# Mamba2 scan and gated feed-forward layer on one core: the first block's steps rearranged, with causal masks on GpSimd for pairs 1 to 3

## The chip, the core and the metric

The kernel runs on one core of a Trainium2 chip. The metric is the time on the device in microseconds (us). Three runs of the kernel before the change took 409.44, 410.94 and 410.81 us, median 410.81.

## What is computed

The reference has two parts. The first is a state-space scan (batch 4, 8 heads, sequence 768, head size 32, state size 16). The reference's chunks are 32 long; any chunk length gives the same sums.

```
log_a = log(clip(a, 1e-6, 1));  cum = cumsum(log_a within a chunk)
L[i,j] = exp(cum[i] - cum[j]) for i >= j, else 0
y      = ((C B^T) * L) x  +  exp(cum) * (C state)
state  = exp(sum log_a) * state + sum_j exp(cum[last] - cum[j]) B_j x_j
```

Its output, 3072 tokens of 256 features, goes into the second part: `xn = y / sqrt(mean(y^2) + 1e-6) * rms_g`, then `silu(xn w_gate) * (xn w_val)`, times `w_out`, with a hidden width of 1536. All weights come in float32.

## The kernel before the change

The 3072 tokens are 12 pairs of 128-token chunks; two pairs make a block of 512 tokens, and there are six blocks. While the feed-forward part of a block runs on TensorE (PE), the scan of the next block is worked out between its matmuls. Block 0 has nothing before it, so its scan (pairs 0 and 1) comes first: this is the lead-in. In it the weights are also brought in: `fetch.k` loads a piece, `pow.k` (ACT, three activations, L182 to L185), `man.k` and `wt.k` (VectorE, DVE, L192, L195, L201) turn it into the form in which it is used. There are 20 pieces: 0 to 3 of 256 columns, 4 to 13 of 512 (gate and value), 14 to 19 of w_out.

**The order is written out by hand.** A long string at the end of the kernel lists steps such as `0:g.0.1/0` (block 0, step g, pair 0, half 1, PSUM slot 0). The kernel emits each step's instructions in that order, and every engine and every DMA queue takes its own in that order. SP issues nearly all DMAs. There are three PSUM slots of two banks (`pair_of_banks`) in the lead-in and two single banks (`bank`), used in turn; a slot is free again when its last reader is done. The raw weights (`wr`) share six buffers.

The steps of a pair, with their lines:

- `aT` (L303) turns a onto tokens, `la0` (L307) clips it, `log`, `log4` (L312, L344) take logarithms. `r` (L355) sums them, `parts` (L362 to L369) splits the sums into three bfloat16 parts, rows.
- `mask` (L422) puts a huge negative number above the diagonal into the bank `e`, by a matmul with a unit matrix. `sums` (L436, L443) adds the sums of logarithms, with small tiles of 32 rows. `exp` (L451) makes the decays L of them. Pairs 0 and 1 have L of 128x1024 for each half of the heads; pairs 2 and 3 work with chunks of 64 and one L of 128x1024.
- `d`, `dx` (L379, L382, L387) are the decays to and from a token; `c`, `cx`, `cc` (L396 to L408) those of whole chunks, of which `cc` makes the column fcol. `scale` (L484) puts them on C and B.
- `turn`, `T`, `Tt` (L499, L507, L1034, L1037) turn B and C, with masks for the two heads of a row tile; `last`, `Tl` (L517, L521) the scaled C.
- `g` (L529; L536 for later pairs) is C B^T: each group of two heads (q = 0 to 3) is one row tile of 32 rows. For pairs 0 and 1 each half has a step of its own, with two row tiles. `L` (L556) multiplies it by the decays.
- `A`, `S` (L582, L596 to L606) are additions to the state and the states. `y` (L623 with the state, L632 within the chunk; L656 for later pairs) is the output, `sq` and `yt` (L695, L712) its squares and its copy to SBUF.

After that `early` (L770) multiplies y by the first gate and value weights before the norm is known, `gate` (L760) does this for normed tokens (`norm` L781, `xn` L741), and from `P` (L844) on products of combined weights and tokens follow, seven where there were eight (`cw` L814, `tx` L821, `two` L890, with `take` L850, `C` L856, `silu` L865, `hid` L869). `o` (L876) and `O` (L934) are the products with w_out. For pairs from 4 on the decays L come by another way: `spread` loads rows of sums by DMA, `sub` (L463) and `ex` (L469) finish them, and GpSimd masks them (L471):

```
        nc.scalar.activation(out=L, in_=L, func=AF.Exp)
        for r in halves:
            nc.gpsimd.affine_select(out=L[r], in_=L[r], pattern=[[0, NH], [1, HC]],
                                    compare_op=ALU.is_ge, fill=0.0, base=0, channel_multiplier=-1)
```

Of the kernel before, what the change touches and what calls it, by code (L numbers as in the profile page):

```python
# [13 lines left out]
BF16 = mybir.dt.bfloat16  # L14
AF = mybir.ActivationFunctionType
# [5 lines left out]
def kernel(  # L21
# [199 lines left out]
    never16 = const.tile([P, HC], BF16, name="never16")  # L221
# [65 lines left out]
    def mask16():  # L287
        for r in halves:
            nc.vector.tensor_copy(out=never16[r], in_=never[r, r])

# [26 lines left out]
    def minus_mid():  # L317
# [19 lines left out]
        "ident16": lambda: nc.vector.tensor_copy(out=ident16, in_=ident), "never16": mask16,  # L337
# [38 lines left out]
    def other_sums():  # L376
# [4 lines left out]
        for k, (r, m) in enumerate((halves, halves[::-1])):  # L381
            nc.tensor.matmul(out=d_ps[m, k, first_four[0], first_four[1]], lhsT=ones[r, m],  # L382
                             rhs=la[(r, *first_four)], start=False, stop=True,
                             tile_position=(r.start, m.start), skip_group_check=True)

    def other_decays():
        nc.scalar.activation(out=d_sb, in_=ps.pop("d"), func=AF.Exp)  # L387

# [3 lines left out]
    def chunk_sums():  # L392
        ps["c"] = full_ps = bank("full_ps", (P, NG * NH))
        n = NC * BH
        for u in range(2):
            nc.tensor.matmul(out=full_ps[:, u * n:u * n + n], lhsT=chunk_ones[:, u], rhs=laf,  # L396
                             start=(u == 0), stop=True, skip_group_check=True)
        nc.tensor.matmul(out=full_ps[:, 2 * n:].rearrange("p (c h) -> p c h", h=NH), lhsT=ones,
                         rhs=la[(slice(0, P), *first_four)], start=False, stop=True,
                         skip_group_check=True)  # L400

    def chunk_decays():
        nc.scalar.activation(out=full.rearrange("p g h -> p (g h)"), in_=ps.pop("c"), func=AF.Exp)
# [15 lines left out]
    def mask(p, e):  # L419
        m = [P, 4, P] if p < 2 else [P, NH, HC]  # L420
        for i in range(2):
            nc.tensor.matmul(out=e[:, i], lhsT=ident16,  # L422
                             rhs=(whole16 if p < 2 else never16).unsqueeze(1).to_broadcast(m),
                             start=True, stop=False, skip_group_check=True)

    def sums(p, half, e):
# [5 lines left out]
        row = rows[p // 2]  # L432
        for k, h in enumerate(heads):
            for i, r in enumerate(rows_of):
                for u in parts:
                    nc.tensor.matmul(out=e[u, i, k * n:(k + 1) * n],  # L436
                                     lhsT=sel[r, h:h + 1].to_broadcast([32, n]),
                                     rhs=row[r, 0, u], start=False, stop=False,
                                     tile_position=(r.start, u.start), skip_group_check=True)
        hs = slice(heads[0], heads[-1] + 1)  # L440
        for i, r in enumerate(rows_of):
            for u in parts:
                nc.tensor.matmul(out=e[u, i], lhsT=row[r, 1, u],  # L443
                                 rhs=sel[r, hs].unsqueeze(2).to_broadcast([32, len(heads), n]),
                                 start=False, stop=True, tile_position=(r.start, u.start),
                                 skip_group_check=True)

    def decay(p, half, e):
        pair_tile(2 * p)
        L = Ls[p][:, :, 4 * half:4 * half + 4] if p < 2 else Ls[p]  # L450
        nc.scalar.activation(out=L.rearrange("p i h m -> p i (h m)"), in_=e, func=AF.Exp)  # L451

# [88 lines left out]
    def products(p, half, g):  # L541

        ps["g", p, half] = g
        product(p, [(2 * half + k, g[:, k]) for k in range(2)])

    def products_at_once(p, g):

        ps["g", p, 0] = g
        ps["g", p, 2], ps["g", p, 3] = g2, g3 = bank("g2", (P, 512)), bank("g3", (P, 512))
# [63 lines left out]
    def first_outputs(p, y):  # L613
# [4 lines left out]
        def inter(i, opens):  # L618
            S, CdT = state[2 * (2 * p + i) - 1], s["T"][:, i, 3]
            for q in range(NQ):  # L620
                r = slice(32 * q, 32 * q + 32)
                o = 64 * (q % 2)
# [3 lines left out]
                    start=opens, stop=True, tile_position=(32 * q, o),  # L626
                    skip_group_check=True)

        def intra(i, opens):
            for h in range(NH):  # L630
# [3 lines left out]
                    rhs=Ls[p][:, i, h], start=opens, stop=True,  # L634
                    tile_position=(0, o), skip_group_check=True)

        if p:
            inter(0, True)
        intra(0, p == 0)
        intra(1, False)  # L640
# [677 lines left out]
```

## Time and profile before

| | |
|---|---|
| median of the runs | 410.81 us |
| the profiled execution | 409.49 us |
| its span, first to last instruction | 407.4 us |
| PE busy | 399.9 us (98%) |
| DVE busy | 303.7 us (75%) |
| ACT busy | 231.9 us (57%) |
| GpSimd (POOL) busy | 37.5 us (9%) |
| first `early` matmul | at 26.18 us |

Matmuls overlap one another, so a PE that counts as busy is not always at its peak. Times of instructions are given as start and length in us from the span's start. "x8" in a timeline line means eight instructions put together, and [0.96 <-...] that the engine stood idle for 0.96 us before, and what seems to have released it.

### The profile page before, as it was taken

To read this page: it belongs to the slowest core of one execution; us is meant where nothing else is said; L and a number is where in the kernel's file an instruction comes from. 1 tells how busy PE (TensorE), PEld (TensorE's weight loads), DVE (VectorE), ACT (ScalarE), POOL (GpSimd) and SP (SyncE) were. 2 spreads that over 40 slices of the span, in tenths; PEclk is the share of its full clock that TensorE was granted. 3 is DMA by queue.
4 is the path that set the end of the run, shared out by engine and by line. 5 is a ranking of instruction groups with operands and counts; after the bars stand their busy time and mean duration, and the time that the engine had idled before them with its cause. 6 is when DMAs were issued, how large, how long until landed. Compare 5 with 4: busy or idle time off the path is not lost.

```text
span 407.4 us, 9550 instructions
## 1 busy us (share of the span) xinstructions
PE 399.9 (98%) x3867; PEld 340.4 (84%) x3867; DVE 303.7 (75%) x698; ACT 231.9 (57%) x506; POOL 37.5 (9%) x61
## 2 busy tenths in 40 slices
PE   8999999999899999999999999999999999999997
PEld 4566577888688899888899988899988899988997
DVE  5999999898976787856799278779455777265863
ACT  3899989795556445664584355534566442453500
POOL 4010000003200001300023000001300000000000
PEclk9999999999999999999999999999999999999999
DMA  9998937400401171302080501020300000100001
GB/s 112 231 213 173 266 118 209 53 0 5 75 0 28 29 126 39 44 1 55 20 131 8 79 2 53 2 80 2 77 2 0 2 4 0 53 1 2 0 2 52
DMA packets 87371, 23.91 MB, mean 59 GB/s; under 512 B 76800, under 2 KB 81152, under 8 KB 87328
## 3 DMA queue, kind: packets, MB, share of 16 engines
q1 hardware_dynamic: 83168, 23.05, 26.9%
q10 hardware_dynamic: 4160, 0.26, 0.8%
q8 instruction: 30, 0.49, 0.5%
q14 instruction: 13, 0.11, 0.1%
HBM read 20.02 MB, written 3.28 MB: 57 GB/s over the span
## 4 chain that ended last, share of the span: by engine, by line
PE 90%; DVE 4%; ACT 3%; DMA 1%; issue 1%; SPq 0%; ACTq 0%
PE gate L844 27%; PE o L934 22%; PE val L844 20%; PE o L876 4%; PE gate L760 3%; PE y L656 3%; PE tp L499 2%; PE gate L770 2%; PE g L536 1%; PE ms L725 1%; DVE sw L814 1%; DVE s L907 1%; DMA L<-rowd 1%; PE e L422 1%; ACT e L183 1%
## 5 line engine op out<-in xcount | busy, mean ns | idle before, releaser
L856 DVE TENSOR_TENSOR c<-val,p 128x512 f32<-128x512 f32 x99 | 67.6, 688 | 46.3 <-PE val L844 27.5
L850 ACT COPY p<-gate 128x512 f32<-128x512 f32 x99 | 57.4, 586 | 52.4 <-PE gate L844 49.2
L844 PE MATMUL gate<-tx,sw 128*128 128x256 f32 x264 | 65.5, 381 | 0.0
L865 ACT ACTIVATE c<-c 128x256 f32<-128x256 f32 x99 | 39.9, 417 | 41.8 <-DVE c L856 41.6
L844 PEld LDWEIGHTS gate<-tx,sw 128*128 128x128 f32 x264 | 49.1, 190 | 7.0 <-ACT p L850 0.3
L869 DVE TENSOR_TENSOR h<-c 128x256 f32<-128x256 f32 x99 | 41.4, 433 | 17.4 <-ACT c L865 17.3
L844 PE MATMUL val<-tx,sw 128*128 128x256 f32 x132 | 33.9, 381 | 1.2 <-DVE c L856 1.2
L844 PE MATMUL val<-xn,wgv 128*128 128x256 f32 x132 | 34.1, 380 | 0.0
L844 PE MATMUL gate<-xn,wgv 128*128 128x256 f32 x132 | 34.0, 382 | 0.0
L844 PE MATMUL val<-xn,sw 128*128 128x256 f32 x132 | 33.9, 381 | 0.0
L844 PE MATMUL gate<-tx,wgv 128*128 128x256 f32 x132 | 33.8, 383 | 0.0
L471 POOL TENSOR_SCALAR_AFFINE_SELECT L<-L 64x512 f32<-64x512 f32 x32 | 23.5, 734 | 83.3 <-ACT L L469 72.9
L934 PEld LDWEIGHTS o<-two,s 128*128 128x128 f32 x240 | 28.3, 192 | 1.9 <-issue 1.4
L934 PE MATMUL o<-wo,h 128*128 128x128 f32 x240 | 29.5, 275 | 0.0
L934 PE MATMUL o<-two,s 128*128 128x128 f32 x240 | 29.3, 276 | 0.1
L934 PEld LDWEIGHTS o<-wo,h 128*128 128x128 f32 x240 | 28.4, 192 | 0.7 <-DVE h L869 0.2
L934 PE MATMUL o<-two,h 128*128 128x128 f32 x240 | 28.9, 275 | 0.0
L844 PEld LDWEIGHTS val<-tx,sw 128*128 128x128 f32 x132 | 24.7, 190 | 5.0 <-DVE c L856 1.6
L844 PEld LDWEIGHTS gate<-tx,wgv 128*128 128x128 f32 x132 | 24.4, 190 | 4.2 <-ACT p L850 0.6
L934 PEld LDWEIGHTS o<-two,h 128*128 128x128 f32 x240 | 27.8, 192 | 0.0
L844 PEld LDWEIGHTS val<-xn,wgv 128*128 128x128 f32 x132 | 24.5, 190 | 3.9 <-DVE c L856 0.6
L844 PEld LDWEIGHTS val<-xn,sw 128*128 128x128 f32 x132 | 24.6, 190 | 3.5 <-DVE h L869 0.2
(179 smaller groups left out, 645.9 us busy)
## 6 DMA issues: line engine op xcount, KB each, us to landing
L<-rowd SPq DMA_DIRECT2D x32, 128.0 KB, 3.2
xr<-in_x_dram SPq DMA_DIRECT2D x24, 128.0 KB, 4.2
wr<-in_moe_w_out_dram SPq DMA_DIRECT2D x6, 512.0 KB, 5.0
wr<-in_moe_w_gate_dram SPq DMA_DIRECT2D x5, 512.0 KB, 5.8
wr<-in_moe_w_val_dram SPq DMA_DIRECT2D x5, 512.0 KB, 5.9
out_dram<-ob SPq DMA_DIRECT2D x9, 256.0 KB, 2.2
br<-in_B_dram SPq DMA_DIRECT2D x22, 64.0 KB, 3.8
cr<-in_C_dram SPq DMA_DIRECT2D x22, 64.0 KB, 3.1
```

What stands on the lines that cost most here:

```text
L471: nc.gpsimd.affine_select(out=L[r], in_=L[r], pattern=[[0, NH], [1, HC]], compare_op=ALU.is_ge, fill=0.0, base=0, channel_multiplier=-1)
L499: nc.tensor.transpose(out=tp[:, k], in_=src[:, i].rearrange("p h n -> p (h n)"), identity=ident)
L656: nc.tensor.matmul(out=y[2 * k + u][rows, i * HC:(i + 1) * HC], start=(k, u, rows.start) not in opened, stop=True, skip_group_check=True, ...
L760: nc.tensor.matmul(out=gv[:, k], lhsT=w[:, t, fs], rhs=xns[0][:, t], start=(t == 0), stop=(t == 1))
L770: nc.tensor.matmul(out=gv[:, k, tk], lhsT=w[:, t, fs], rhs=yts[0][:, t, tk], start=(s == 0 and t == 0), stop=(t == 1), skip_group_check=True)
L844: nc.tensor.matmul(out=dst[:, half[w]], lhsT=lhsT, rhs=rhs, start=(k in (1, 2, 5) and w == 0), stop=True, skip_group_check=True)
L850: nc.scalar.copy(out=t, in_=Xs[j])
L856: nc.vector.tensor_tensor(out=t, in0=Zs[j], in1=a, op=ALU.add)
L865: nc.scalar.activation(out=u, in_=src[:, half[0]], func=AF.Silu)
L869: nc.vector.tensor_tensor(out=hidden_tile(blk, j)[:, c // 10 - 1, c % 10 - 1], in0=u, in1=src[:, half[1]], op=ALU.mult)
L876: nc.tensor.matmul(out=o, lhsT=hs_[blk, f // 2][:, f % 2, k // 2, (k % 2) * P:(k % 2 + 1) * P], rhs=wo[:, f], start=opens, stop=(f == NF - ...
L934: nc.tensor.matmul(out=o[t] if apart else o[:, t * P:(t + 1) * P], lhsT=lhsT[:, t], rhs=rhs, start=(k in (1, 2, 4, 5) and j == 0 and (apar ...
```

## The change

1. For pairs 0 and 1, `g` is one step: the products of all four row tiles of a pair, into two PSUM slots.
2. Only pair 0 is masked by matmuls. For pairs 1 to 3 `mask` is left out, the first matmul of `sums` opens the bank, and a new step `keep` sets the upper triangle of L to zero on GpSimd after `exp`: two selects of 128x512 for each half of pair 1, four of 64x512 for pairs 2 and 3. In `sums` the two kinds of matmul change places. The bfloat16 mask of 64 columns, never16, is gone.
3. The two matmuls in `d` and the one in `c` that join half chunks for pairs 0 and 1 are gone; GpSimd multiplies the decays instead (`dd`, and one product in `cx`).
4. In `y` of pairs 0 and 1 all products with the state come ahead of those within the chunk. Pair 1's additions (`A.1`) are done at the end of `y.0`, into a part of its bank.
5. `T` and `Tt` of pair 0 are made by ACT instead of DVE.
6. The order is new, in all six blocks. In the lead-in `aT` stands between pair 0's two masks; `fetch.18`, `x.3` stand earlier, `bc.3`, `bc.4` and `bc.5` in other places, `rowout.1` ahead of `fetch.8`; `scale.2` stands behind `yt.0`. Around the border to block 1, `sub.8` to `sub.10`, `cw.2` and `two.0` stand behind more of block 1's products. Blocks 1 to 5 have the same steps as before in another sequence.

The diff's core, with the order up to the first products of pair 3:

```diff
-        for k, (r, m) in enumerate((halves, halves[::-1])):
-            nc.tensor.matmul(out=d_ps[m, k, first_four[0], first_four[1]], lhsT=ones[r, m],
-                             rhs=la[(r, *first_four)], start=False, stop=True,
-                             tile_position=(r.start, m.start), skip_group_check=True)
...
+    def of_other_half():
+        for u, r in enumerate(halves[::-1]):
+            first = d_sb[(r, u, *first_four)]
+            nc.gpsimd.tensor_tensor(out=first, in0=first, in1=first_groups(r, u), op=ALU.mult)
...
     def chunk_sums():
-        ps["c"] = full_ps = bank("full_ps", (P, NG * NH))
         n = NC * BH
+        ps["c"] = full_ps = bank("full_ps", (P, 2 * n))
         for u in range(2):
             nc.tensor.matmul(out=full_ps[:, u * n:u * n + n], lhsT=chunk_ones[:, u], rhs=laf,
                              start=(u == 0), stop=True, skip_group_check=True)
-        nc.tensor.matmul(out=full_ps[:, 2 * n:].rearrange("p (c h) -> p c h", h=NH), lhsT=ones,
-                         rhs=la[(slice(0, P), *first_four)], start=False, stop=True,
-                         skip_group_check=True)
+
+    def first_groups(r, u):
+        return full[r, 0:NG - 4].rearrange("p (u c b) h -> p u c b h", u=2, b=NB)[:, u, 0:4, 0]
...
-        nc.scalar.activation(out=full.rearrange("p g h -> p (g h)"), in_=ps.pop("c"), func=AF.Exp)
+        nc.scalar.activation(out=full[:, 0:NG - 4].rearrange("p g h -> p (g h)"),
+                             in_=ps.pop("c"), func=AF.Exp)
+        nc.gpsimd.tensor_tensor(out=full[:, NG - 4:], in0=first_groups(slice(0, P), 0),
+                                in1=first_groups(slice(0, P), 1), op=ALU.mult)
...
-    def mask(p, e):
-        m = [P, 4, P] if p < 2 else [P, NH, HC]
+    def mask(e):
         for i in range(2):
             nc.tensor.matmul(out=e[:, i], lhsT=ident16,
-                             rhs=(whole16 if p < 2 else never16).unsqueeze(1).to_broadcast(m),
+                             rhs=whole16.unsqueeze(1).to_broadcast([P, 4, P]),
                              start=True, stop=False, skip_group_check=True)
...
+        hs = slice(heads[0], heads[-1] + 1)
+        for i, r in enumerate(rows_of):
+            for u in parts:
+                nc.tensor.matmul(out=e[u, i], lhsT=row[r, 1, u],
+                                 rhs=sel[r, hs].unsqueeze(2).to_broadcast([32, len(heads), n]),
+                                 start=p > 0, stop=False, tile_position=(r.start, u.start),
+                                 skip_group_check=True)
...
-                                     rhs=row[r, 0, u], start=False, stop=False,
+                                     rhs=row[r, 0, u], start=False, stop=True,
...
-        hs = slice(heads[0], heads[-1] + 1)
-        for i, r in enumerate(rows_of):
-            for u in parts:
...
+    def keep_causal(p, half):
+        n = P if p < 2 else HC
+        hs = slice(4 * half, 4 * half + 4) if p < 2 else slice(0, NH)
+        for r in [slice(0, P)] if p < 2 else halves:
+            L = Ls[p][r, :, hs]
+            for i in range(2):
+                nc.gpsimd.affine_select(
+                    out=L[:, i], in_=L[:, i], pattern=[[0, hs.stop - hs.start], [1, n]],
+                    compare_op=ALU.is_ge, fill=0.0, base=0, channel_multiplier=-1)
...
-    def products(p, half, g):
-
-        ps["g", p, half] = g
-        product(p, [(2 * half + k, g[:, k]) for k in range(2)])
-
-    def products_at_once(p, g):
+    def products_at_once(p, g, g2=None):
 
         ps["g", p, 0] = g
-        ps["g", p, 2], ps["g", p, 3] = g2, g3 = bank("g2", (P, 512)), bank("g3", (P, 512))
+        if g2 is None:
+            ps["g", p, 2], ps["g", p, 3] = g2, g3 = bank("g2", (P, 512)), bank("g3", (P, 512))
+        else:
+            ps["g", p, 1] = g2
+            g2, g3 = g2[:, 0], g2[:, 1]
         product(p, [(0, g[:, 0]), (1, g[:, 1]), (2, g2), (3, g3)])
...
-        def inter(i, opens):
+        for i in range(p == 0, 2):
             S, CdT = state[2 * (2 * p + i) - 1], s["T"][:, i, 3]
             for q in range(NQ):
-                r = slice(32 * q, 32 * q + 32)
-                o = 64 * (q % 2)
+                r, o = slice(32 * q, 32 * q + 32), 64 * (q % 2)
                 nc.tensor.matmul(
                     out=y[o:o + 64, q // 2, i * P:(i + 1) * P],
                     lhsT=S[r].rearrange("p t d -> p (t d)"), rhs=CdT[r],
-                    start=opens, stop=True, tile_position=(32 * q, o),
+                    start=(i == (p == 0)), stop=True, tile_position=(32 * q, o),
                     skip_group_check=True)
-
...
+                    rhs=Ls[p][:, i, h], start=False, stop=True,
                     tile_position=(0, o), skip_group_check=True)
-
-        if p:
-            inter(0, True)
-        intra(0, p == 0)
-        intra(1, False)
-        inter(1, False)
+        if p == 0:
+            additions(1, [y[:, 0, 2 * P:3 * P].rearrange("p (i t d) -> p i t d", i=2, t=2)])
         del st[p], Ls[p]
...
-        mask(p, e)
+        if p == 0:
+            mask(e)
...
-        "sums": lambda p, half=0: sums(p, half, ps["e", p, half]),
+        "sums": lambda p, half=0: (p and start_decays(p, half), sums(p, half, ps["e", p, half])),
+        "keep": lambda p, half=0: keep_causal(p, half),
...
+        "d": other_sums, "dx": other_decays, "dd": of_other_half,
...
-        "T": lambda p, i: turned(p, i, ac.copy if p else dv.tensor_copy),
-        "Tt": lambda p, i, t: turned_of(p, i, t, by_scalar if p else by_vector),
+        "T": lambda p, i: turned(p, i, ac.copy),
+        "Tt": lambda p, i, t: turned_of(p, i, t, by_scalar),
...
-        "g": lambda p, half: products(p, half, take("g", ("g", p, half))),
+        "g": lambda p: products_at_once(p, take("g", ("g", p, 0)), take("g", ("g", p, 1))),
...
     order = """
-        0:warm 0:a 0:set 0:bc.0 0:bc.1 0:x.0 0:x.1 0:ident 0:fetch.0 0:ones 0:zeros 0:fetch.1 0:upto
-        0:gcol 0:never 0:after 0:fetch.2 0:mid 0:ident16 0:whole16 0:fetch.3 0:idle.7 0:mask.0.0/1
-        0:mask.0.1/0 0:hmask 0:part 0:part2 0:fetch.4 0:head 0:mids 0:fetch.5 0:bc.2 0:x.2 0:fetch.6
-        0:aT 0:la0 0:log4.0.4 0:fetch.7 0:log 0:mask.1.1/2 0:log4.4.2 0:log4.6.2 0:sel 0:upto2
-        0:after2 0:whole 0:r.0 0:tmask 0:parts.0 0:middles 0:c*2 0:turn.0.1 0:T.0.1 0:cx 0:kinks
-        0:eps 0:Tt.0.1.0 0:d 0:dx 0:fetch.8 0:Tt.0.1.1 0:sums.0.1 0:exp.0.1 0:turn.0.0 0:Tt.0.0.0
-        0:T.0.0 0:Tt.0.0.1 0:scale.1 0:cc 0:sums.0.0 0:exp.0.0 0:mean 0:turn.1.0 0:never16 0:g.0.1/0
-        0:L.0.1 0:turn.1.1 0:bc.3 0:T.1.1 0:Tt.1.0.1 0:Tt.1.1.1 0:Tt.1.0.0 0:T.1.0 0:Tt.1.1.0
-        0:fetch.9 0:sums.1.1 0:exp.1.1 0:g.0.0/1 0:scale.0 0:last.0 0:Tl.0 0:L.0.0 0:pow.0 0:man.0
-        0:A.0 0:S.0 0:bc.4 0:row.1 0:rowout.1 0:man.1 0:wt.0 0:g.1.1/0 0:A.1 0:S.1 0:last.1 0:pow.1
-        0:L.1.1 0:Tl.1 0:pow.2 0:mask.1.0/2 0:sums.1.0 0:exp.1.0 0:row.0 0:g.1.0/1 0:mask.3/0
-        0:pow.5 0:man.5 0:fetch.10 0:r.1 0:y.0/2 0:sq.0 0:pow.3 0:L.1.0 0:y.1/1 0:sq.1 0:wt.1
-        0:scale.2 0:rowout.0 0:man.2 0:pow.6 0:yt.0 0:ydone.0 0:turn.2.0 0:early.0.0/2 0:parts.1
-        0:sums.3 0:exp.3 0:ms.0 0:rs.0 0:wt.2 0:pow.4 0:yt.1 0:ydone.1 0:early.0.1 0:mask.2/0
-        0:sums.2 0:turn.2.1 0:man.3 0:wt.5 0:wt.3 0:early.1.0/1 0:early.1.1 0:man.4 0:fetch.11
-        0:man.6 0:fetch.14 0:scale.3 0:exp.2 0:pow.7 0:xn.0 0:wt.6 0:T.2.0 0:T.2.1 0:Tt.2.1.0
-        0:Tt.2.1.1 0:Tt.2.0.0 0:Tt.2.0.1 0:table.0 0:x.3 0:wt.4 0:gate.2/0 0:man.8 0:man.7
-        0:fetch.13 0:norm.0 0:norm.1 0:wt.7 0:gg.2/2 0:L1.2.3 0:L1.2.2 0:silu.0 0:hid.0 0:L.2.0
-        0:tx.0 0:gate.3/1 0:pow.9 0:silu.2 0:hid.2 0:man.9 0:fetch.15 0:A.2 0:S.2 0:pow.8 0:wt.8
-        0:silu.3 0:hid.3 0:wt.9 0:pow.10 0:man.11 0:cw.3 0:gate.4/2 0:silu.4 0:hid.4 0:man.10
-        0:pow.11 0:wt.11 0:turn.3.1 0:turn.3.0 0:T.3.0 0:Tt.3.0.1 0:T.3.1 0:Tt.3.0.0 0:Tt.3.1.1
-        0:Tt.3.1.0 0:wt.10 0:switch.0 0:P.1.3 0:take.1.3 0:x.4 0:gate.5/1 0:silu.5 0:hid.5
...
+        0:warm 0:a 0:set 0:bc.0 0:mean 0:bc.1 0:x.0 0:x.1 0:ident 0:fetch.0 0:ones 0:zeros 0:fetch.1
+        0:upto 0:gcol 0:never 0:after 0:fetch.2 0:mid 0:fetch.5 0:ident16 0:eps 0:whole16 0:fetch.3
+        0:idle.7 0:mask.0.0/2 0:hmask 0:part 0:part2 0:fetch.4 0:head 0:sel 0:mids 0:aT 0:mask.0.1/0
+        0:upto2 0:after2 0:whole 0:tmask 0:la0 0:log4.0.4 0:r.0*2 0:parts.0 0:log 0:c*2 0:cx
+        0:log4.6.2 0:turn.0.1 0:T.0.1 0:Tt.0.1.0 0:Tt.0.1.1 0:d 0:dx 0:dd 0:scale.1 0:cc 0:x.3
+        0:turn.0.0 0:T.0.0 0:Tt.0.0.1 0:Tt.0.0.0 0:kinks 0:scale.0 0:sums.0.1 0:exp.0.1 0:log4.4.2
+        0:sums.0.0 0:exp.0.0 0:turn.1.0 0:turn.1.1 0:T.1.1 0:T.1.0 0:Tt.1.0.0 0:Tt.1.1.0 0:Tt.1.0.1
+        0:Tt.1.1.1 0:g.0/10 0:L.0.0 0:L.0.1 0:bc.2 0:man.0 0:sums.1.1/2 0:exp.1.1 0:keep.1.1 0:A.0
+        0:S.0 0:fetch.18 0:man.2 0:last.1 0:pow.0 0:wt.0 0:sums.1.0/1 0:exp.1.0 0:keep.1.0 0:g.1/02
+        0:L.1.1 0:man.1 0:last.0 0:Tl.0 0:y.0/1 0:S.1 0:x.2 0:middles 0:row.1 0:rowout.1 0:r.1
+        0:fetch.8 0:pow.1 0:wt.1 0:Tl.1 0:row.0 0:L.1.0 0:man.5 0:fetch.6 0:pow.2 0:wt.2 0:fetch.11
+        0:sq.0 0:pow.5 0:y.1/2 0:sq.1 0:x.4 0:pow.4 0:pow.3 0:yt.0 0:ydone.0 0:early.0.0/0 0:wt.5
+        0:man.3 0:fetch.7 0:rowout.0 0:ms.0 0:rs.0 0:yt.1 0:ydone.1 0:early.0.1 0:parts.1 0:sums.3/1
+        0:exp.3 0:sums.2/2 0:exp.2 0:keep.2 0:man.4 0:wt.3 0:scale.2 0:turn.2.1 0:turn.2.0 0:T.2.0
+        0:Tt.2.0.1 0:Tt.2.1.0 0:T.2.1 0:Tt.2.1.1 0:Tt.2.0.0 0:pow.6 0:xn.0 0:wt.4 0:man.6
+        0:early.1.0/1 0:early.1.1 0:table.0 0:norm.0 0:silu.0 0:norm.1 0:man.8 0:tx.0 0:pow.7
+        0:hid.0 0:gate.2/2 0:silu.2 0:pow.8 0:A.2 0:S.2 0:wt.6 0:hid.2 0:man.7 0:bc.3 0:scale.3
+        0:wt.7 0:gate.3/0 0:silu.3 0:hid.3 0:fetch.10 0:fetch.9 0:pow.9 0:man.9 0:gg.2/1 0:L1.2.2
+        0:L.2.0 0:L1.2.3 0:wt.8 0:wt.9 0:gate.4/2 0:silu.4 0:hid.4 0:turn.3.1 0:switch.0 0:turn.3.0
+        0:pow.11 0:cw.3 0:T.3.0 0:Tt.3.1.1 0:Tt.3.0.0 0:Tt.3.0.1 0:Tt.3.1.0 0:T.3.1 0:man.11
+        0:man.10 0:gate.5/1 0:silu.5 0:hid.5 0:bc.5 0:wt.11 0:pow.10 0:wt.10 0:bc.4 0:P.1.3
+        0:take.1.3 0:keep.3 0:fetch.12 0:pow.12 0:y.2/2 0:S.3 0:yt.2 0:sq.2 0:ydone.2 0:P.6.3
+        0:take.6.3 0:fetch.13 0:pow.13 0:man.13 0:P.1.4 0:switch.1 0:P.2.4 0:P.2.3 0:man.12 0:gg.3/2
+        0:L.3.0 0:L1.3.3 0:L1.3.2 0:P.7.3 0:silu.1 0:scale.4 0:y.3/2 0:C.11.3 0:P.5.3 0:silug.11.3
+        0:take.7.3 0:P.4.3 0:fetch.15 0:wt.12 1:S.0 0:yt.3 0:sq.3 0:ydone.3 0:tok 0:silug.21.3
...
```

## Prediction

> **What bounds the kernel now.** I read the page first, then the busy times by stage, then the chain of work, then the timelines of the places where the chain leaves the tensor engine. The page's first part says that PE is busy for 98% of the span, but that figure is pipelined, so the stages say more (stretch, then length and busy time with the instructions of PE, PEld, DVE, ACT and POOL, the granted clock, the DMA share, GB/s):
>
> ```profile
> 10.00:26.20 16.20, 14.17 (x208) 8.92 (x206) 15.21 (x38) 14.90 (x31) 0.73 (x1) 1.00 0.95 240
> 26.20:63.00 36.80, 36.75 (x514) 23.27 (x514) 35.87 (x81) 33.64 (x62) 1.46 (x2) 1.00 0.73 173
> 63.00:94.00 31.00, 31.00 (x143) 26.55 (x144) 28.34 (x61) 24.89 (x48) 0.73 (x1) 1.00 0.39 85
> 94.00:106.30 12.30, 11.07 (x54) 9.41 (x52) 11.11 (x18) 8.89 (x18) 6.06 (x8) 1.00 0.31 60
> 106.30:407.40 301.10, 298.29 (x2906) 267.23 (x2906) 207.40 (x471) 146.54 (x344) 23.64 (x32) 1.00 0.15 30
> ```
>
> From 106.3 on PE is idle for 2.8 us of 301; nothing that the change does to the first block makes that part shorter, and a new order of the same steps has at most those 2.8 us and the switches between tile shapes to win. From 26.2 to 63 PE is full **and DVE too** (35.87 of 36.80 us): the two race. From 63 to 94 DVE has 2.7 us of slack. Two places show DVE winning the race against PE. The first is the start of the feed-forward part (timeline):
>
> ```profile
> 25.18 0.86 DVE L712 TENSOR_SCALAR yt<-y,gcol 128x256 f32<-128x256 f32 x2
> 26.18 1.97 PE L770 MATMUL gate<-yt,wgv 128*128 128x256 f32 x8 [0.96 <-ACT sq L695]
> ```
>
> The page blames ACT, but the first gate product reads yt, whose second half ends at 26.04. The other is the chain between 60 and 63 us: PE goes on when DVE has worked off its list.
>
> ```profile
> 60.22 0.33 DVE Cd L484
> 60.55 0.34 DVE Bd L484
> 60.89 0.60 DVE c L856
> 61.49 0.60 DVE wgv L201
> 62.09 0.21 DVE A L596
> ```
>
> Last, the border to block 1: here PE stands for 1.23 us behind one DVE queue (combined weights, L814 and L890).
>
> ```profile
> 97.16 0.42 DVE L814 TENSOR_TENSOR sw<-wgv 128x256 f32<-128x256 f32 x1
> 98.17 6.51 POOL L471 TENSOR_SCALAR_AFFINE_SELECT L<-L 64x512 f32<-64x512 f32 x8 [33.84 <-ACT L L469]
> 100.14 0.87 DVE L814 TENSOR_TENSOR sw<-wgv 128x256 f32<-128x256 f32 x1
> 106.28 1.13 PE L844 MATMUL val<-tx,sw 128*128 128x256 f32 x4 [1.23 <-DVE c L856]
> ```
>
> The same DVE operation takes 0.42 us at 97.16 and 0.87 while POOL runs its masks.
>
> **What the skill says.** "SBUF — State Buffer", section "Who interferes with whom": a DVE instruction with two SBUF inputs and a GpSimd instruction that reads SBUF exclude each other for the whole instruction; one PSUM input frees DVE of that. The trace agrees: +0.45 us on each sw. "TensorEngine Tiling (Array Packing)", "Key Properties": tiles work independently, and a change of tiling drains the array. The trace agrees with both. The timeline's L623, four row tiles of 32, is 16 matmuls of 128 columns in 0.68 us, so a group of four costs about 0.14, no more than one; L529, two row tiles, is 8 matmuls of 256 columns in 1.13, so 0.22 for a pair. A change of tiling costs about 0.09 (L623 to L632 starts 0.09 later than the columns need).
>
> **The change part by part.** All sums are against the profiled execution: 409.49 us, span 407.4, so 2.1 us outside it. The median shown is 410.81, 1.3 above.
>
> *Products C·Bᵀ.* 16 matmuls for a pair at once, four by four: 4 groups x 0.22 + 0.1 = 1.0 us, against 2 x 1.0 now (1.13 less the drain). That is 1.0 us of PE for each of two pairs, before 26 us, where PE has idle time anyway (14.17 of 16.20 busy): worth it only as far as L (L556) starts earlier. It costs a tie: both halves wait for two PSUM slots. The new order inside sums and y saves three or four changes of tiling at 0.09, also before 26: nothing by itself.
>
> *Masks.* Of 12 mask matmuls (L422) pair 0 keeps four; the eight of pairs 1 to 3 go, two in 0.43 us once PE runs fast (20.71 to 21.14 in the timeline): 1.7 us of PE, of which only pair 2's 0.43 lies after 26.2. GpSimd gets 12 selects of 512 columns: two for each half of pair 1, four for pairs 2 and 3. L471 does 8 in 6.51, 0.81 each beside DVE, and two in 1.45, 0.72 each, at 163.94. They have 64 partitions; 128 with as many columns is not shown, I take the same 0.8 (bounds 0.7, and 1.6 for double). Pair 1's 1.6 us for each half stand between exp (L451) and the product with L, but DVE gets to that product only after a mantissa, S.0, another mantissa and a weight (0.66 + 0.75 + 0.66 + 0.34 = 2.4 us), which hide them; without that cover 1.6 us. Pairs 2 and 3 run back to back, 6.5 us, just when DVE makes xn and weights. **Price to DVE**: 0.45 for each select that meets an operation with two SBUF inputs: 0 to 12 x 0.45 = 5.4 us. Normed, L and most hidden products read PSUM and don't meet; in the order after the two exps I count two that do (a weight, a mantissa), 0.9 us.
>
> *Lighter DVE, other engines.* The six T copies of pair 0 go to ACT (1.6 us at 0.27), never16 goes (0.33): -1.9 for DVE, +1.6 for ACT. Two small matmuls of d and one of c go (0.26 and 0.15), POOL multiplies instead (0.2 to 0.4 each), ahead of the product for fcol, which is needed first by S.1, 8 us later.
>
> *A turned first.* a's data land at 3.2; aT starts at 4.42 behind four mask matmuls (1.91 us). With two ahead it starts near 3.5. But la0 then stands behind whole, tmask and others on DVE, to about 4.8 against 5.30: 0.5 us earlier. Through r, parts (1.7) and exp this gives L of pair 0 at about 12.3 in place of 13.05, and its second half 1.4 us sooner, since both products are there.
>
> *A new wait.* Pair 1's additions go into the bank of y.0. S.1 on DVE now waits for y.0's end (about 20.1 by the chain exp.1.0, Tl.0, then y of 2.6 us), and behind it are queued rowout.1, a weight, L.1.0, a mantissa and wt.2, and then yt.0: 0.24 + 0.34 + 1.15 + 1.07 + 0.34 = 3.1. DVE stands 0.6 us there. With S.1 0.85: yt.0 starts at 20.1 + 0.85 + 3.1 = 24.1 in place of 25.18, and the gate product at 25.1: **1.1 us earlier**.
>
> *DMAs.* On SP x.3 and the w_out piece 18 move ahead, the loads bc.3 to bc.5 back, and rowout.1, which waits for DVE (about 21), stands ahead of pieces 8, 6 and 11. They then start at 21 to 23; before, 6 to 8 start at 20.6 to 21.9 and land 5.3 to 6.8 later. Piece 6 is needed near 34: no cost; if that cover went, up to 2 us. Piece 18 holds one of six buffers for long; piece 9 waits for piece 6's use (about 36), lands about 41, and is needed at 46.
>
> *From yt.0 to the C of 60.89.* DVE's list is the same but for wt.2, which leaves (-0.34), and scale.2 and rowout.0, which enter (+0.68 + 0.24). So C comes 35.71 (60.89 - 25.18) + 0.58 + 0.9 (collisions) = 37.2 us after yt.0, at 24.1 + 37.2 = **61.3, which is 0.4 later than now**. PE's start 1.1 us earlier and its 0.43 saved are used up by waits for DVE between 42 and 62 us (gate.4 for its weights, the product of pieces 10 and 11).
>
> *The border.* From there to P.7.1 of block 1 the new order has 5.5 us less on DVE (sub.8, sub.9, sub.10 1.8, cw.2 1.4, two.0 1.4, C and hidden 0.9: moved behind). That is more than PE stands there and the 0.4 together, and between 63 and 94 DVE has its 2.7 of slack. PE's eight matmuls from 103.16 need 1.73 and the next starts at 106.28: 1.4 us of standing go. Bounds -1.4, and 0 if what is moved behind makes PE wait later; I take **-1.4**.
>
> *Blocks 1 to 5*: the same steps in another order, 0, from -1 to +1.5.
>
> Sum: +0.4 - 1.4 = -1.0: 408.5 from the profiled execution, 409.8 from the median. The runs shown (409.44 to 410.94) have room for both; I take the middle, 410.15 - 1.0 = **409.1**.
>
> **The rivals.** A (faster): the selects run while DVE reads PSUM and collide hardly at all. Then C comes at 60.4, 0.5 earlier than now, pair 2's mask saves its 0.43 behind it, the border 1.4, and a quarter of the 2.8 us of idle time after 106 goes with the new order: -0.5 - 0.4 - 1.4 - 0.7 = -3.0, 407.1 from the same middle. For it: POOL is idle then, norm and hidden read PSUM; against: xn, weights and mantissas stand there. B (slower): **the selects of GpSimd hold DVE's port.** All 12 meet: 5.4 in place of 0.9, C at 65.8, 4.9 later than now; PE, which is full afterwards, never makes it good: +4.9 - 1.4 = +3.5, 413.6. It decides for slower (+2) once 0.45n - 0.5 - 1.4 is over 2, from 9 of the 12 selects on. For it: 6.5 us of POOL in the fullest stretch of DVE; against: half of DVE's time there reads PSUM. C (no effect): PE's savings lie where DVE bounds, and the order of blocks 1 to 5 gives back the border: about 0, 410.2.
>
> **Chances.** This kernel's measurement can tell about 0.5% (2 us) from no change. Forecast with C, within that: 0.46 (407.8 to 411 by itself). A: 0.38. B: 0.12, and 0.04 for waits of over 2 us in all in the newly ordered blocks. The range reaches over A to 405.5 (A with all but 0.5 of the 2.8 us of idle time gone), and into B, to 412.5.
>
> **What would show it.** Right: first gate product near 25; L's first product near 12.3; the C of 60.89 near 61.3; selects of 0.7 to 0.8 us at 32 to 38 with DVE's L195 and L201 there 0.4 longer; no PE wait over 1 us near 105. Wrong: DVE with idle time from 26 to 60, a PE wait of over 2 us anywhere after 106, or L.1.1 waiting for POOL.

## The result, and the profile after

The changed kernel takes 412.13 us (median of 18 runs, 410.46 to 412.42), the kernel before 409.50 us beside it (18 runs): ratio 1.0042, 95% interval 1.0028 to 1.0057. It is slower by 0.42%: less than the 0.5% that I called no change, and inside the range, but the other way than forecast. Most runs of the kernel before lie in two groups, ten near 409.4 us and seven near 410.8, and of the changed kernel's three lie near 410.5 and twelve near 412.2, so that it is 1.2 to 1.4 us slower from group to group. One difference between executions shows in the first 10 us: the two matmuls of `r` (L355, now L350) took 0.67 us in the profiled execution of the kernel before and 1.19 us in the changed kernel's, and all that hangs on them starts later. So I compare stretches that begin at the first early gate product, not times of single executions.

The busy times by stage of the changed kernel's profiled execution (411.13 us, span 409.1), columns as before:

```profile
10.00:26.20 16.20, 12.86 (x214) 8.88 (x210) 15.31 (x35) 15.52 (x33) 6.54 (x12) 1.00 0.96 216
26.20:63.00 36.80, 34.53 (x474) 21.09 (x474) 35.19 (x76) 31.81 (x59) 7.54 (x9) 1.00 0.85 212
63.00:94.00 31.00, 30.80 (x189) 25.96 (x172) 27.66 (x61) 25.69 (x49) 0.72 (x1) 1.00 0.14 43
94.00:106.30 12.30, 12.30 (x58) 10.83 (x57) 9.08 (x21) 5.83 (x12) 1.23 (x2) 1.00 0.00 1
106.30:409.10 302.80, 298.97 (x2911) 267.45 (x2909) 208.82 (x475) 151.22 (x354) 28.22 (x39) 1.00 0.17 34
```

PE has less work (14.17 down to 12.86 before 26 us), but from 26.2 to 63 it was busy for 36.75 us and now for 34.53 of 36.80: PE has got waits there. POOL went from 1.46 to 7.54 us in that stage, the selects. The start of the feed-forward part (timeline):

```profile
23.88 0.87 DVE L713 TENSOR_SCALAR yt<-y,gcol 128x256 f32<-128x256 f32 x2
24.41 1.99 PE L771 MATMUL gate<-yt,wgv 128*128 128x256 f32 x8 [0.71 <-DVE yt L713]
```

It is 1.77 us earlier than before. That understates the new beginning: in the profile of the run with pow.10 moved (below), which has the same steps up to here and whose matmuls of L350 took 0.67 us as before, this product starts at 23.74, 2.44 us earlier. In all profiles with these steps it starts between 23.74 and 25.61.

The chain of work up to the C that was at 60.89 (start, length, what):

```profile
53.39 0.67 ACT e L182
...
54.84 0.72 ACT e L185
55.56 0.48 ACT p L851
...
56.09 1.99 PE gate L845 x8
58.09 1.73 PE val L845 x8
59.81 0.73 PE g L544 x32
...
62.56 0.60 DVE c L857
```

Before, VectorE's list ended in that C, and VectorE had no wait over 0.2 us between 26 and 63 us; now the chain comes from ScalarE: three operations of pow.10, then take.1.3 (p), behind which PE's P.6.3 and the products up to pair 3's g are late. The C is 1.67 us later, 62.56 for 60.89. The ledger, from the two profiled executions (C by the timelines, 60.81 and 62.48):

| | before | after | |
|---|---|---|---|
| first early gate product | 26.18 | 24.41 | -1.77 |
| from there to the C | 34.63 | 38.07 | +3.44 |
| from the C to the end | 346.59 | 346.62 | +0.03 |
| span | 407.4 | 409.1 | +1.7 |

The first row depends on how the execution began (above); the others repeat better. The new beginning works; more than it brings is lost before 62 us; and the tail as a whole gives nothing, though the border to block 1 improved. Three theories. **1**: the selects hold VectorE. **2**: the new order of steps makes engines wait. **3**: what is moved at the border, and the new order of blocks 1 to 5, costs what the border gains.

### The profile page after: what moved, and what is told of

It reads as the page before. It is cut to its first block, busy times and chain, and to the rows that moved or that the text cites. A ratio compares the mean times of both kernels' runs of the same rounds, so it can differ in the third digit from the quotient of the medians.

```text
span 409.1 us, 9551 instructions
## 1 busy us (share of the span) xinstructions
PE 398.2 (97%) x3855; PEld 339.2 (83%) x3855; DVE 301.3 (74%) x690; ACT 233.8 (57%) x513; POOL 47.9 (12%) x76
## 4 chain that ended last, share of the span: by engine, by line
PE 80%; DVE 13%; ACT 3%; issue 2%; DMA 1%; SPq 0%; DVEq 0%; ACTq 0%
PE gate L845 26%; PE val L845 20%; PE o L935 19%; PE o L877 5%; PE y L657 3%; PE g L544 1%; DVE L L563 1%; PE tp L507 1%; DVE wgv L201 1%; DMA wr<-in_moe_w_gate_dram 1%; PE gate L761 1%; PE ms L726 1%; DVE s L911 1%; DVE m L195 1%; DVE tx L822 1%
## 5 line engine op out<-in xcount | busy, mean ns | idle before, releaser
L479 POOL TENSOR_SCALAR_AFFINE_SELECT L<-L 64x512 f32<-64x512 f32 x32 | 23.5, 734 | 85.2 <-ACT L L477 45.1
L704 POOL TENSOR_TENSOR sq<-sq 128x256 f32<-128x256 f32 x10 | 7.6, 761 | 180.0 <-issue 134.4
L951 ACT COPY v<-o 128x256 f32<-128x256 f32 x15 | 5.6, 372 | 40.2 <-PE o L935 40.2
```

The costliest lines, as they stand in the source:

```text
L704: nc.gpsimd.tensor_tensor(out=sqs[blk][:, tk], in0=s2[:, 0], in1=s2[:, 1], op=ALU.add)
L951: nc.scalar.copy(out=ts[k], in_=halves_of(Os["X"]))
```

## Experiments

Every run is timed against the kernel before on the same chip. "Gate to C" is the row of 34.63 and 38.07 us above in that run's profiled execution, "C to end" the one of 346.6; "order" stands for the list of steps. Both come from one profiled execution for each run. Three executions of the changed order up to the C gave 38.07, 38.06 and 38.05 us; the order before gave 34.63 and 34.62, but 36.12 in a third, where VectorE stood 1.50 us for a late transfer.

**Selects of pairs 2 and 3 taken out.**

```diff
-  ... 0:exp.2 0:keep.2 ... 0:take.1.3 0:keep.3
+  ... 0:exp.2 ... 0:take.1.3
```

> The changed kernel without keep.2 and keep.3: the eight GpSimd selects of pairs 2 and 3 are left out and nothing takes their place, so the part of L above the diagonal of these two pairs stays unmasked. Theory 1 (the selects hold VectorE, about 1.7 us of lengthened VectorE operations between 32 and 39 us, and the lead-in behind them is bound by VectorE): the operations of L192, L195 and tx there go back to 0.42, 0.68 and 0.42 us, the C of 62.5 us starts near 61.0, and the time falls by 1.2 to 2.0 us, to a ratio of 0.999 to 1.002 to the kernel before. Theory 2 (the new order of the steps costs the time, the selects little of it): the C stays at 62.0 or later, and the ratio is 1.003 to 1.005.

This kernel leaves out the masks of two pairs, so it is there to price them only. Ratio 0.9989 (0.9978 to 0.9999), gate to C 36.44 us, 1.63 less. Theory 1 holds. The changed kernel's timeline of POOL and VectorE (start, length, engine, line):

```profile
32.30 6.80 POOL L457 TENSOR_SCALAR_AFFINE_SELECT L<-L 64x512 f32<-64x512 f32 x8 [7.05 <-ACT L L449]
```

```profile
32.86 0.88 DVE L192 TENSOR_SCALAR m<-wr 128x512 int32<-128x512 int32 x1
33.77 1.01 DVE L195 SCALAR_TENSOR_TENSOR m<-wr,m 128x512 f32<-128x512 uint32 x1
34.70 0.68 DVE L782 TENSOR_TENSOR u<-gate,r 128x512 f32<-128x512 f32 x1
...
37.10 0.43 DVE L192 TENSOR_SCALAR m<-wr 128x512 int32<-128x512 int32 x1
37.56 1.01 DVE L195 SCALAR_TENSOR_TENSOR m<-wr,m 128x512 f32<-128x512 uint32 x1
38.50 0.87 DVE L822 TENSOR_TENSOR tx<-xn 128x256 f32<-128x256 f32 x1
39.40 0.42 DVE L822 TENSOR_TENSOR tx<-xn,tx 128x256 f32<-128x256 f32 x1
```

and without the selects:

```profile
33.50 0.42 DVE L192 TENSOR_SCALAR m<-wr 128x512 int32<-128x512 int32 x1
33.95 0.69 DVE L195 SCALAR_TENSOR_TENSOR m<-wr,m 128x512 f32<-128x512 uint32 x1
34.56 0.68 DVE L782 TENSOR_TENSOR u<-gate,r 128x512 f32<-128x512 f32 x1
...
38.04 0.42 DVE L822 TENSOR_TENSOR tx<-xn 128x256 f32<-128x256 f32 x1
```

Four operations are held, 0.46 + 0.32 + 0.32 + 0.45 = 1.55 us. u (gate is in PSUM) isn't, though POOL works through it. L192 has one SBUF input: it is held at 32.86 all the same, and at 37.10, still beside the selects, it isn't.

**The same pairs masked by matmuls again.**

```diff
+  never16; if p in (0, 2, 3): mask(p, e)
-  0:keep.2  0:keep.3
```

> The changed kernel with pairs 2 and 3 masked by matmuls as before (four mask matmuls of 512 columns on TensorE, some 0.9 us, and the two small VectorE copies of never16), the eight selects dropped. Theory 1: VectorE is not held at 32 to 39 us, TensorE has 2.3 us of idle time between 26 and 63 us to take the four matmuls, so 0.7 to 1.7 us come back: ratio 1.000 to 1.0025. Theory 2: no more comes back than the mask matmuls cost: ratio 1.0035 to 1.006.

Ratio 1.0017 (1.0005 to 1.0029), gate to C 37.38: of the 1.63 us the matmuls take 0.94 back (four of them, 0.43 for two). Here the selects are the dearer mask, by 0.7 us of gate to C.

**Selects alone, in the kernel before.**

```diff
-  the mask matmuls of pairs 2 and 3
+  0:exp.2 0:keep.2 ... 0:take.1.3 0:keep.3
```

> The kernel before with one part of the change alone: pairs 2 and 3 masked by GpSimd's selects, each pair's right behind its exp in GpSimd's list, in place of the four mask matmuls (0.9 us of TensorE). Theory 1: the selects (4 x 0.72 us a pair) lengthen the VectorE operations beside them by 1 to 2 us, and the time rises by 0.4 to 1.5 us: ratio 1.001 to 1.004. Theory 2: TensorE loses 0.9 us of work and nothing is held that counts: ratio 0.9975 to 1.000.

The edit also gives `sums` the changed sequence of its matmuls. Ratio 1.0047 (1.0031 to 1.0063): theory 1, and more than it asked for. Its timeline:

```profile
35.80 7.22 POOL L459 TENSOR_SCALAR_AFFINE_SELECT L<-L 64x512 f32<-64x512 f32 x8 [7.39 <-ACT L L451]
```

```profile
35.77 1.74 DVE L201 SCALAR_TENSOR_TENSOR wgv<-m,e 128x512 f32<-128x512 f32 x2
37.43 0.87 DVE L192 TENSOR_SCALAR m<-wr 128x512 int32<-128x512 int32 x1
38.34 1.01 DVE L195 SCALAR_TENSOR_TENSOR m<-wr,m 128x512 f32<-128x512 uint32 x1
39.27 0.88 DVE L192 TENSOR_SCALAR m<-wr 128x512 int32<-128x512 int32 x1
40.19 1.01 DVE L195 SCALAR_TENSOR_TENSOR m<-wr,m 128x512 f32<-128x512 uint32 x1
```

Here five operations meet them, 0.46 + 0.45 + 0.32 + 0.46 + 0.32 = 2.0 us. In that execution PE then waits 1.22 us for ScalarE and 0.50 for VectorE, and its granted clock between 40 and 50 us is 0.83; gate to C is 38.14, 3.51 more than before, so the held operations are not all of it.

**two.0 moved up, to behind cw.1.**

```diff
-  1:C.22.1 1:two.0 1:P.3.1
+  0:cw.1 1:two.0
```

> The changed kernel with two.0 (the four subtractions of L891) moved up in VectorE's list, from behind the second C of block 1 to right behind cw.1, into the 3.3 us in which VectorE stands idle from 104.0 us on. Theory 3 (the queue behind two.0 is what TensorE waits for at 110.96 us): that wait of 0.66 us goes, and the time falls by 0.4 to 0.7 us: ratio 1.0025 to 1.0032. Rival: the next wait is as late (P of L851 or the tables of ScalarE), and the ratio stays at 1.0038 to 1.0046.

Ratio 1.0013 (0.9998 to 1.0027), C to end 345.81, 0.81 less. In the changed kernel:

```profile
108.01 0.81 DVE L891 TENSOR_TENSOR two<-wo 128x256 f32<-128x256 f32 x1
...
111.10 0.68 DVE L857 TENSOR_TENSOR c<-val,p 128x512 f32<-128x512 f32 x1
```

```profile
111.84 1.13 PE L845 MATMUL val<-xn,wgv 128*128 128x256 f32 x4 [0.50 <-DVE c L857]
```

two.0 ran into the block's own selects (L479) and took twice its time, ahead of a C that PE waits for. Moved up it takes 0.42 an operation and PE's wait is gone. Theory 3 holds for the border.

**P.1.3 and take.1.3 ahead of gate.5**, and the same **with matmul masks and two.0 moved**.

```diff
+  0:P.1.3 0:take.1.3 0:gate.5/1 0:silu.5 ... 0:pow.10
-  0:gate.5/1 0:silu.5 ... 0:pow.10 ... 0:P.1.3 0:take.1.3
```

> The changed kernel with P.1.3 and take.1.3 put back ahead of gate.5, where the kernel before has them, so that ScalarE's copy of L851 stands ahead of pow.10 and of silu.5; all else, the selects too, as changed. Theory 2 (part of the loss is the new order: TensorE stands 0.9 us at 55.13 us behind that copy, and VectorE then 0.67 us behind the product g of pair 3): the wait at 55 goes, the C of 62.5 us comes 0.5 to 0.9 us earlier, and the time falls by 0.4 to 1.0 us: ratio 1.0018 to 1.0032. Rival (VectorE's list alone sets the C; the wait of TensorE is hidden behind it): the C moves by less than 0.2 us, ratio 1.0038 to 1.0048.

> The changed kernel with three repairs: pairs 2 and 3 masked by matmuls, P.1.3 and take.1.3 ahead of gate.5, and two.0 behind cw.1. If the three gains stand side by side (0.7 to 1.1 us for the masks, 0.4 to 1.0 us, 0.4 to 1.2 us), the ratio is 0.9965 to 0.999. If they are the same stall seen three times, it stays at 1.000 to 1.002.

Ratios 1.0076 (1.0058 to 1.0093) and 1.0031 (1.0019 to 1.0043): the move costs 1.1 us of gate to C (39.16 for 38.07, 38.47 for 37.38). Theory 2 in this form fell. ScalarE's timeline of the first says why:

```profile
53.07 0.63 ACT L851 COPY p<-gate 128x512 f32<-128x512 f32 x1
55.16 0.60 ACT L787 ACTIVATE u<-gate 128x512 f32<-128x512 f32 x1 [1.46 <-PE gate L761]
55.66 0.78 ACT L182 ACTIVATE e<-wr,kinks 128x512 int16<-128x512 int16 x1
```

The copy is early now, but ScalarE then stands 1.46 us behind gate.5, and pow.10, still behind it, is later than ever. It was not take.1.3 that was badly placed, but pow.10.

**pow.10 ahead of gate.4.**

```diff
+  0:wt.9 0:pow.10 0:gate.4/2
-  0:wt.11 0:pow.10 0:wt.10
```

> The changed kernel with one step moved: pow.10 (three ScalarE operations, 2.2 us) from behind silu.5 up to ahead of gate.4, into the 1.29 us in which ScalarE waits for the gate product at 47.9 us. The run with P.1.3 and take.1.3 moved had shown ScalarE idle and then late with pow.10. If pow.10's place is what makes ScalarE's copy of L851 late, the wait of TensorE of 0.9 us at 55.1 us and VectorE's 0.29 us behind ScalarE go, and the time falls by 0.5 to 1.0 us: ratio 1.0018 to 1.003. Rival (silu.4, now 0.9 us later behind it, holds hid.4 and the product of gate.5, and the loss only moves): 1.0038 to 1.006.

The changed kernel's PE, and ScalarE with pow.10 moved:

```profile
56.09 1.13 PE L845 MATMUL gate<-tx,sw 128*128 128x256 f32 x4 [0.74 <-ACT p L851]
```

```profile
52.97 0.58 ACT L851 COPY p<-gate 128x512 f32<-128x512 f32 x1 [0.19 <-PE gate L845]
```

Gate to C is 37.46, 0.6 less; PE's wait of 0.74 us and VectorE's two (0.29 at 55.60, 0.67 at 60.54) are gone, and VectorE has no wait left between 24 and 68 us. Theory 2 holds in this form. The ratio, 1.0028 (1.0017 to 1.0040), is where it was expected, but its interval overlaps the changed kernel's (1.0028 to 1.0057).

**Lead-ins and tails exchanged at g.0 of block 1.** Each takes one kernel's order to there, and the other's for the steps left.

```diff
+  order of one kernel up to 1:g.0, then the other's
```

> The kernel before with its own order up to g.0 of block 1 (at about 113 us) and the changed kernel's order of the remaining steps of blocks 1 to 5 behind it. Forecast on record for that order: nothing, ratio 0.9988 to 1.0012. Theory 3 (the new order of blocks 1 to 5 costs part of the loss; the trace shows 0.3 us of waits at 219 and 0.6 us at 224 that the kernel before lacks): ratio 1.0015 to 1.003.

> The changed kernel with its own order up to g.0 of block 1 (at about 116 us) and the kernel before's order of the remaining steps of blocks 1 to 5 behind it: the complement of the run that gave the kernel before the changed tail. Theory 3 (the changed order of blocks 1 to 5 costs some 1.3 us by itself, wherever the lead-in ends): the waits at 219 and 224 us go, and the time falls by 0.7 to 1.4 us from the changed kernel's: ratio 1.0008 to 1.0025. Rival (the tail's cost stands only behind the old lead-in): 1.0036 to 1.0048.

The old lead-in with the new tail: 1.0035 (1.0023 to 1.0046), C to end 348.01, 1.42 more; 0.54 of it is a new wait of PE for a C (L856) at the join, at 111.56 us. The new lead-in with the old tail: 1.0033 (1.0023 to 1.0044), C to end only 0.28 less than changed; two executions with the same steps behind the C (the runs with repairs below) differ by 0.30. So the new tail costs 1.4 us behind the old lead-in, more than was expected, and a cost behind its own isn't shown by this pair. One wait in it that the old tail lacks (changed kernel, PE):

```profile
225.00 1.13 PE L845 MATMUL val<-xn,wgv 128*128 128x256 f32 x4 [0.41 <-DVE ob L962]
```

**The new beginning with the old order behind it.**

```diff
+  changed order up to 0:early.0.0, then the old order, pairs 2 and 3 masked by matmuls
```

> The changed kernel's functions and order up to the first early gate product, with GpSimd masking pair 1 alone; from there the kernel before's order of the steps, with matmul masks on pairs 2 and 3. It prices the new beginning by itself. Forecast of the sum: the early gate product comes 1.1 us earlier and nothing behind it is longer: ratio 0.9965 to 0.9985. Theory 1 says the same, since the selects beside VectorE's weight work are gone. Rival (the beginning's gain is lost again because the transfers of fetch.7, fetch.9 and fetch.10 that it puts later, or VectorE's list, set the end of the lead-in anyway): ratio 0.999 to 1.002.

Ratio 1.0145 (1.0126 to 1.0165), which doesn't price the beginning: the old order puts turn.2.0 ahead of the first gate product, where PE waits 2.40 us for VectorE, and then names slot 2 for early.0.0, which in the new beginning y.1 holds until yt.1 has read it: 1.70 us more. Later VectorE stands 5.36 us for a late transfer (cr, at 38.79 us). The beginning can't be had without the order behind it; with it, it is 1.77 us in the ledger (2.44 with like first matmuls).

**All masks by matmul.**

```diff
-  0:keep.1.0 0:keep.1.1 0:keep.2 0:keep.3      + mask(p, e) for every pair
```

> The changed kernel with all masks by matmul (pair 1 too): no selects are left. Beside the run with pairs 2 and 3 masked by matmuls (1.0017) it prices the four selects of pair 1 (0.7 us each, VectorE operations at 15.2 and 17.4 us lengthened by 0.75 us in all) against four mask matmuls of 512 columns (some 0.9 us of TensorE). Theory 1: VectorE's list sets the first product of 26 us, and 0.2 to 0.7 us come back: ratio 1.0000 to 1.0012. Rival (TensorE's added work stands on the same path): 1.002 to 1.0035.

Ratio 1.0027 (1.0014 to 1.0040), inconclusive. A weight piece came late in this execution, and VectorE stood 1.54 us for it. In the changed kernel the selects of pair 1 do hold VectorE, L195 at 15.21 us (0.73 us for 0.42) and L201 at 17.40 (0.86 for 0.41); what that costs in time stays open. It is the cover that the prediction named for piece 6, and it isn't safe.

**Repairs together**: matmul masks, pow.10, two.0, old tail; then with more.

```diff
+  0:pow.10 0:gate.4/2;  0:cw.1 1:two.0;  old order from 1:g.0;  mask(p, e) for pairs 2, 3
```

> The changed kernel with four repairs: matmul masks on pairs 2 and 3, pow.10 ahead of gate.4, two.0 behind cw.1, and the kernel before's order of blocks 1 to 5 from g.0 of block 1. If the four gains add (1.0, 0.6, 0.6 and 1.2 us off the changed kernel's 1.0042), the ratio is 0.9945 to 0.9975; if pow.10 gives nothing, 0.9965 to 0.999.

Ratio 1.0000 (0.9986 to 1.0013), above both expectations. The gains don't add: matmul masks with pow.10 give gate to C 37.52, no less than pow.10 with the selects (37.46). VectorE waits 0.85 us for the early product behind the masks.

```diff
-  0:man.13 ... 0:man.12 0:gg.3 ... 0:C.11.3
+  0:gg.3 ... 0:C.11.3 0:man.13 0:man.12
```

> The changed kernel with pow.10 ahead of gate.4 and with man.13 and man.12 (two pairs of L192 and L195, 2.1 us of VectorE) moved behind the C of 61 us; the selects stay. If VectorE's list sets the C, it starts 1.5 to 2.1 us earlier after the first early gate product than in the run with pow.10 alone (35.4 to 36.0 us behind it, not 37.5), and the time falls by 0.5 to 1.5 us more: ratio 0.9992 to 1.0016. If TensorE has taken over, the C moves by less than 0.8 us and the ratio stays at 1.002 to 1.003.

> The run with four repairs (matmul masks on pairs 2 and 3, pow.10, two.0, the old order of the tail: ratio 1.000) and two more: man.13 and man.12 behind the C, and the two mask matmuls of pair 3 put ahead of the row sums, where TensorE waits 0.4 us at 26 us. If VectorE's list is the bound: ratio 0.995 to 0.998. If TensorE is: 0.998 to 1.0005.

> As the run before it, but with GpSimd's selects on pairs 2 and 3 in place of the matmul masks. Theory 1 with VectorE's list the bound: the selects cost 1.0 to 1.6 us of the list that stands behind nothing else, against 0.9 us of TensorE: ratio 0.002 above that run or more. If TensorE is the bound by now, the selects are the cheaper mask: ratio equal or down to 0.002 below it.

Ratios 1.0075 (1.0049 to 1.0101), 1.0047 (1.0029 to 1.0065), 1.0072 (1.0050 to 1.0094), all slower. The last can't price the selects against the matmuls of the one before it, since VectorE stood 1.06 us for a late transfer in its profile. VectorE's timeline of the first:

```profile
60.39 0.69 DVE L563 TENSOR_TENSOR L<-g,L 128x512 f32<-128x512 f32 x1 [2.33 <-PE g L544]
...
62.93 0.42 DVE L192 TENSOR_SCALAR m<-wr 128x512 int32<-128x512 int32 x1
```

The 2.1 us taken out of VectorE's list turn into 2.33 us of waiting for pair 3's g, and gate to C falls by 0.2 only: **VectorE's list and PE's were equally long**. Behind the C the moved work then stands ahead of pair 3's states, and C to end grows by 2.4.

```diff
-  0:P.1.4 0:switch.1 0:P.2.4 0:P.2.3 ... 0:gg.3/2
+  0:early.0.0/0 0:mask.3/1;  0:P.1.4 0:switch.1 0:P.2.3 ... 0:gg.3/2 0:P.2.4
```

> The run with four repairs (ratio 1.000) with the mask matmuls of pair 3 ahead of the row sums and P.2.4 (0.87 us of TensorE) behind the product g of pair 3, as the kernel before has it; man.13 and man.12 stay where the changed kernel has them. If TensorE's list up to that product is the bound there, the C comes 0.8 to 1.6 us earlier behind the first early gate product (35.9 to 36.7 us, not 37.5) and the ratio is 0.996 to 0.9985. If VectorE's list is, the C stays at 37 us or later and the ratio at 0.999 to 1.001.

Gate to C 36.44, as expected; ratio 1.0011 (0.9994 to 1.0029), above the expected one and no better than 1.0000 within the intervals. C to end is 345.86, for 345.56 in the run with four repairs, whose steps from the C on are the same. No version of the changed kernel that keeps all masks beat the kernel before.

**The kernel before, two.0 moved back.**

```diff
-  1:cw.2 1:two.0 1:P.2.0
+  1:C.22.1 1:two.0 1:two.4
```

> The kernel before with two.0 moved back in VectorE's list, from ahead of the C of 105.55 us to behind the C of C.22.1. In the kernel before TensorE stands 1.39 us at 104.67 us behind that C, which waits for cw.2 and two.0, themselves stretched by GpSimd's selects of 98.2 to 104.7 us (0.87 us for a subtraction that takes 0.42 us alone). If two.0 is what holds the C, the wait falls by 1.0 us or more and the ratio is 0.9965 to 0.9985; if the next C or P is as late, 0.999 to 1.001.

Ratio 0.9986 (0.9976 to 0.9996), C to end 345.70, 0.89 less; PE's wait of 1.23 us is gone, and one of 0.31 at 110.99 us has come. It is the only version with all its masks that beats the kernel before, by 0.14%: at the border more was to be had by moving one step than the change's -0.73.

## Why the prediction was wrong

**The beginning: right, too small.** Forecast 1.1 us earlier, measured 1.77, and 2.44 with like first matmuls. L of pair 0 starts at 12.62 (forecast 12.3; 11.97 with like matmuls), yt.0 at 23.88 (24.1; 23.21). Some 0.5 us is a cause that I missed, and the gain from it was luck. It lies in "the first gate product reads yt, whose second half ends at 26.04". The old order gives y.0 and early.0.0 the same slot, 2, so the product must wait until all of y.0 is read, 1.00 us after yt.0's start. In the new one y.0 has slot 1 and early.0.0 slot 0, and the product starts 0.53 us after yt.0, when yt's first operation is done. This is argued from the orders and times; no run moved the slot alone, but the run with the old order behind the new beginning shows such a wait. Whether the last read was yt's (26.04) or, as the page has it, ScalarE's sq stays open.

**From yt.0 to the C: the step that failed.** Forecast 0.58 (list) and 0.9 (two collisions), so 1.48 us more than before; measured 38.60 for 35.63, so 2.97 more.

- *Collisions, mis-sized*: "I count two that do (a weight, a mantissa), 0.9 us". Four were held, 1.55 us in VectorE's timeline and 1.63 in gate to C. The weight (L201 at 32.25, 0.68 us) wasn't. Of the mantissa (man.6) both operations were, and behind it the L195 of man.8 and the first L822, which stood among the steps behind and read two SBUF inputs; so I counted too few even by that rule. L192 I had left out as having one input. The same section of the Trainium skill ("SBUF — State Buffer", "Who interferes with whom") lists `tensor_scalar` too, as able to enter a mode that takes the shared ports; the trace agrees at 32.86 (0.88 us for 0.42), but at 37.10 it took 0.43. A held operation cost 0.32 to 0.46 us, near the 0.45 that I took; a select cost 0.2 us of the path on average (1.63 / 8), since most met PSUM readers.
- *ScalarE's list, missed*: I worked out the lists of VectorE and PE only. pow.10 stands behind silu.5 and ahead of take.1.3, and makes PE wait: 0.6 us (the run with pow.10 moved).
- The remaining 0.7 us is near the 0.58 forecast for scale.2 and rowout.0, if the three add; no run shows that, and matmul masks and pow.10 did not add. P.2.4 ahead of g.3 (0.87 us of PE) may be in it; no run moved it alone.

So C came 1.67 us late, not 0.4. Rival B's mechanism was at work, with four held operations beside the last eight selects and 1.6 us, not with the 9 of 12 that it asked for; with matmul masks in their place the kernel is still slower (1.0017), because other waits join them. Rival C was right on one point: the order of blocks 1 to 5 gave back the border, +0.03 from the C to the end.

**The border: half.** Forecast -1.4, bounded by "0 if what is moved behind makes PE wait later". The wait of 1.23 us behind the C went, but one of 0.50 behind two.0, which is what was moved behind, took its place: -0.73.

**Blocks 1 to 5: forecast 0, from -1 to +1.5.** With -0.73 at the border and +0.03 from the C to the end they cost 0.76 by difference, inside that range. The run with two.0 moved up has the new tail and no wait at the border, and its C to end (345.81) is 0.45 above the kernel before without its 1.23 us (345.36). So 0.45 to 0.76 is an estimate; the exchanged tails give 0.3 and 1.4. The wait at 225 us is 0.41 of it. Which steps cost the rest was not tried.

**Sum**: -1.77 + 3.44 - 0.73 + 0.76 = +1.7, against -1.0. With the beginning's 2.44 it would be +1.0, an estimate from two profiles. The size of each loss is small; together they changed the sign.

## What to carry to other kernels

Where two engines are equally loaded, price a moved step on every engine's list, ScalarE's too: what leaves one list turns into a wait for the other, as the 2.1 us of mantissas did. Before work is given to GpSimd, go through VectorE's operations in that stretch one by one and ask which read SBUF only; and where a wait has no clear releaser, look for a PSUM slot that two steps share. A long hand-made order can be priced by exchanging halves of it, though the join brings waits of its own (0.54 us here); and a single step moved (two.0) may bring as much as a large change (0.89 us at the border).

## What the hardware showed that I had not expected

GpSimd's select on 128x512 takes 0.70 to 0.72 us, as long as on 64x512 (0.72 each at 163.94 us before): twice the partitions cost nothing. This agrees with the Trainium skill, "GPSIMD Engine Reference", section 5.1, where each core works on 16 partitions of its own. VectorE's single-input mask of integers (L192) can be held by a select as long as the first L822 with two inputs, 0.46 and 0.45 us; of two in the changed kernel one was.

Waits of PE that add up to about 2 us can be followed by a lower clock. In the kernel before with selects, six products L770 take 4.51 us behind two waits (1.22 and 0.50 us; eight took 3.67 before them). The granted clock is 0.63 from 29 to 36 us in the run with the old order behind the new beginning (waits of 2.40 and 1.70 us), and 0.72 from 66 to 72 in the run with matmul masks and man.13 and man.12 moved (a wait of 2.21 us ahead of 65.50). But in the run with pow.10 and these two moved, a wait of 2.35 us ahead of 67.64 left it at 1.00. The Trainium skill, "TensorE: Matmul & The Clock Gate", section "What's actually happening", says that the clock is halved after an idle window of about 3.4 us of a counter that runs freely. Each of these waits is shorter than that window, so the window alone doesn't account for the three cases; what decides between them and the fourth stays open. So a wait can cost more than its length, in some executions only.
